# Loading one branch's output weights in 20 pieces instead of one in a two-branch attention decode kernel

## The chip, the cores and the metric

The kernel runs on one core of a Trainium2 chip. The core has five engines with their own instruction streams: TensorE (PE in the profile, its weight loads PEld), VectorE (DVE), ScalarE (ACT), GpSimd (POOL) and SyncE (SP), and sixteen DMA engines that move data between the chip's memory (HBM) and the core's buffer (SBUF, 128 partitions). SP computes nothing here; it only issues loads. The metric is the device time of one execution in microseconds, lower is better; several executions are timed and the median is given.

## The reference, cut to what matters

Two attention branches, A and B, each decode one token for a batch of two: 32 heads of width 128 over a cache of 4096 keys and values, then an output projection. A gate mixes the two results. Everything is in 32-bit floats. The two branches have separate caches and weights but share the input `A_x`.

```python
def branch(x, k_cache, v_cache, wq, wo):          # x [2, 1, 512]
    q = (x @ wq).reshape(2, 1, 32, 128).transpose(0, 2, 1, 3)
    scores = einsum("bhqd,bhkd->bhqk", q, k_cache) * 128 ** -0.5
    p = softmax(scores)
    o = einsum("bhqk,bhkd->bhqd", p, v_cache)     # caches [2, 32, 4096, 128]
    return o.transpose(0, 2, 1, 3).reshape(2, 1, 4096) @ wo    # wo [4096, 512]

g = sigmoid((x * gate_w).sum(-1, keepdims=True))
out = g * branch_A + (1 - g) * branch_B
```

The four caches are 134 MB each and the four weight matrices 8.4 MB each, so about 570 MB are read once.

## The kernel before

A unit is one group of four heads of one batch entry; a branch has 16 of them, and there are 32 in all. A unit's keys and its values are 8.4 MB each: 128 partitions, each with 128 tokens of 128 numbers, which lie one behind the other in HBM (64 KB for a partition). There are three such buffers: `kt[0]` and `kt[1]` take turns for the keys, `vt` holds the values. The query weights come before the first unit and the output weights after the last ones, through the same `kt` buffers.

For each unit VectorE multiplies the keys with the query in place and sums over the width (L391, L394), finds the maxima, ScalarE takes the exponentials (L365), and TensorE multiplies them with the values (L369). The loops of a branch run over pairs of units, one for each `kt` buffer. At the end of a branch the heads are gathered and scaled, and TensorE multiplies them with the output weights: branch A's in `project_out` (L489, products on L497) into the accumulator `most`, while the last unit of branch B is still under way; branch B's in `project_out` for the first 28 of 32 rows and in `project_last` (L508, products on L512) for the last four.

All large loads are issued by SP in an order that is written out (from L516): query weights A, keys 0, query weights B, keys 1, values 0, and then keys and values in turn. The last entries are keys 31, values 30, output weights A (`load_wo("A")`, L524), values 31, output weights B. `S.dma` (L97) issues one load and returns the semaphore count that says it has landed; each load adds 16 to the semaphore of its slot. Before a load SP waits until its buffer is free: for the output weights of A until VectorE is through with keys 30 (`k_free`), for values 31 until ScalarE reports that TensorE is through with values 30 (`v_free`), for the output weights of B until VectorE is through with keys 31. SP's instructions run strictly in order, so a load that is held up holds up those behind it.

The output weights are laid out as `(p r) e -> p r e`: partition p holds 32 rows (`OR`) of 512 numbers, 2 KB each, and these 32 rows lie one behind the other in HBM. `load_wo` (L243) loads branch A's in one piece, slot `f`, and branch B's in six pieces, slots `abchij`, with 16, 8, 4, 2, 1 and 1 rows of each partition. `parts` keeps the counts to wait for; `arrived` (L213) makes an engine wait for them. For branch A `project_out` waits once, for `parts["wo", "A"][0]`, ahead of its first product. The values of the last unit come in three pieces of 64, 48 and 16 tokens of each partition, and `last_products` (L381) waits for each in turn.

The end of the kernel: TensorE's products with branch B's output weights, a copy of the accumulator by ScalarE (L609), a product that folds it in (L612), copies out (L620, L621) and two small stores.

Of the kernel before, what the change touches and what calls it, by code (L numbers as in the profile page):

```python
# [12 lines left out]
P = 128  # L13
B = 2
# [14 lines left out]
OR = H * DH // P  # L29
DQ = DH // OR  # L30
EARLY = OR - 4
OS = 2
SCALE = DH ** -0.5

QUARTERS = [slice(j * PH, (j + 1) * PH) for j in range(G)]

# [9 lines left out]
class Streams:  # L46
# [32 lines left out]
    def put(self, e, make, reads=(), writes=(), gives=None):  # L79

        self.before(e, reads, writes)
        i = make(self.engines[e])
        if gives is not None:
            i.then_inc(gives, 1)
            return None
        self.ticks[e] += 1
        i.then_inc(self.sems[e], 1)
        point = self.sems[e], self.ticks[e]
        self.after(point, reads, writes)
        return point  # L90
# [51 lines left out]
def tile_gated_decode(ctx: ExitStack, tc: tile.TileContext, ins: dict, out: bass.AP):  # L142
# [12 lines left out]
    slot = small.tile([P, VC], F32, name="slot")  # L155
# [23 lines left out]
    with tc.tile_critical():  # L179
        S = Streams(nc, tc)  # L180
# [27 lines left out]
        parts = {}  # L208

        def load_parts(item, t, src, slots, *cuts):  # L210
            parts[item] = [S.dma("sp", t[:, i:j], src[:, i:j], slot=s) for s, i, j in zip(slots, cuts, cuts[1:])]
# [31 lines left out]
        def load_wo(n):  # L243
            i = place["wo", n]
            nc.sync.wait_ge(k_free[i], NU // 2)
            t = kt[i].rearrange("p r d -> p (r d)").rearrange("p (r e) -> p r e", e=D)
            for r in r_kt[i]:
                r.writers, r.readers = [], []
            load_parts(("wo", n), t, ins[n + "_wo"].rearrange("(p r) e -> p r e", p=P), *(
                ("f", 0, OR) if n == "A" else ("abchij", 0, OR // 2, 3 * OR // 4, EARLY, OR - 2, OR - 1, OR)))  # L250


        class Scratch:
# [8 lines left out]
        rows, ident, ones, xg, w, e = start(D), start(P), start(1), start(B * KC), start(P), start(1)  # L262
# [3 lines left out]
        def vput(e, make, reads=(), writes=(), **kw):  # L266
# [6 lines left out]
                                  slot="y"))  # L273
# [51 lines left out]
        def project(n):  # L325
# [20 lines left out]
            for i, t in enumerate(qa):  # L346
                half = slice(i * STRIPS * DH, (i + 1) * STRIPS * DH)
                mark(put("act", lambda x: x.activation(qrow[:, half], t.rearrange("p g d -> p (g d)"), AF.Copy, scale=SCALE),  # L348
                         [r_qa[i]], [r_qrow[i]]))
# [137 lines left out]
        wo = {}  # L487
# [33 lines left out]
        for u in range(2, NU):  # L521
            load_k(u)
            load_v(u - 1)
        load_wo("A")  # L524
        load_v(NU - 1)
        load_wo("B")

        spread_queries(0)
        for h in (0, 1):
            t = kt[0][:, h * NS // 2:(h + 1) * NS // 2]  # L530
            r = R()
# [84 lines left out]
        for i, e in enumerate(("dve", "act")):  # L616
            for j in range(STRIPS // OS):
                k = (i * STRIPS // OS + j) * QT
                src = acc[i][k:k + B, :D // STRIPS]
# [27 lines left out]
```

## Time and profile before

| what | value |
|---|---|
| median of 3 timed runs | 1324.44 us (1324.32 to 1324.47) |
| the profiled execution | 1324.58 us |
| its span (first to last instruction in the trace) | 1322.8 us |
| VectorE busy | 1166.3 us (88%) |
| TensorE busy | 343.3 us (26%) |
| ScalarE busy | 101.4 us (8%) |
| bytes read from HBM | 570.43 MB, 431 GB/s over the span |
| granted TensorE clock, mean | 0.627 |

The page of the profile lists the busy time of each engine, the span in 40 slices, the DMA queues, the chain of work that ended last and the costliest groups of instructions. Further views of the same trace give the busy time in chosen stretches, each engine's instructions in order of time, and who waited for whom. An engine's idle time costs nothing unless the chain that ends last passes through it. The DMA share of a stretch is the mean busy share of the sixteen DMA engines; in a very short stretch it can come out above 1.

### The profile page before, as it was taken

The page shows a single profiled execution, that of the slowest core. Times are in us where ns is not written, and L with a number is a line of the kernel's source. Part 1 is how long each engine was busy: PE and PEld are TensorE (multiplying, and loading weights), DVE is VectorE, ACT ScalarE, POOL GpSimd, SP SyncE. Part 2 cuts the span into 40 slices and gives each one's busy share as a digit, 9 for nine tenths or more (in the row PEclk, how much of TensorE's full clock was granted, in tenths as well). Part 3 has the DMA queues.
Part 4 walks back from the last instruction along what each step waited for, and adds up shares of the span by engine and source line. Part 5 has one row for each costly group of instructions (what it writes and reads, how often), then busy time and mean ns, then how long its engine had stood idle before and what let it go on. Part 6 is the DMA issues. An engine that isn't in the chain of part 4 may idle for free. (4 is left out here: it accounts for less than half of the span.)

```text
span 1322.8 us, 6257 instructions
## 1 busy us (share of the span) xinstructions
PE 343.3 (26%) x2406; PEld 100.7 (8%) x2406; DVE 1166.3 (88%) x321; ACT 101.4 (8%) x331; POOL 1.2 (0%) x8
## 2 busy tenths in 40 slices
PE   3202222202222221222224022222212222221256
PEld 0000000000000000000002000000000000000012
DVE  2399999999999999999999899999999999999960
ACT  0000000001010000101000010100001010000100
POOL 0000000000000000000000000000000000000000
PEclk9656666556666655666665566666566666656668
DMA  9999999999999999999999999999999999999998
GB/s 412 442 414 442 442 416 442 444 414 444 442 430 428 442 442 416 442 442 416 444 442 419 438 442 434 426 440 440 420 440 440 420 442 442 426 432 442 434 420 357
DMA packets 11109, 570.53 MB, mean 431 GB/s; under 512 B 1239, under 2 KB 1243, under 8 KB 1630
## 3 DMA queue, kind: packets, MB, share of 16 engines
q1 hardware_dynamic: 11092, 570.43, 99.6%
q8 instruction: 4, 0.07, 0.0%
q14 instruction: 3, 0.02, 0.0%
q10 hardware_dynamic: 10, 0.01, 0.0%
HBM read 570.43 MB, written 0.00 MB: 431 GB/s over the span
## 5 line engine op out<-in xcount | busy, mean ns | idle before, releaser
L391 DVE TENSOR_TENSOR kt<-kt,q 128x16384 f32<-128x16384 f32 x31 | 534.0, 17226 | 56.1 <-DVEq L95 56.0
L394 DVE TENSOR_REDUCE sc<-kt 128x128 f32<-128x16384 f32 x31 | 533.8, 17220 | 1.1
L369 PE MATMUL vp<-vt,pr 128*32 128x512 f32 x2048 | 291.8, 733 | 919.3 <-PEq L95 918.5
L369 PEld LDWEIGHTS vp<-vt,pr 128*32 128x32 f32 x2048 | 80.3, 132 | 1129.3 <-issue 1126.9
L365 ACT ACTIVATE pr<-sc,nm 32x128 f32<-32x128 f32 x128 | 50.9, 398 | 160.0 <-ACTq L95 118.2
L431 ACT ACTIVATE pr<-nil 128x512 f32<-128x512 f32 x31 | 19.3, 624 | 426.4 <-ACTq L95 426.4
L452 ACT ACTIVATE vs<-vp,slot 128x128 f32 (+1 forms) x16 | 5.9, 368 | 451.6 <-ACTq L95 451.6
L339 PE MATMUL qa<-kt,cols 128*2 128x512 f32 x128 | 18.7, 741 | 22.9 <-DMA kt<-in_B_wq_dram 15.7
L365 ACT ACTIVATION_READ_ACCUMULATOR pr<-sc,nm (+1 forms) x128 | 23.5, 184 | 0.0
L350 DVE STREAM_TRANSPOSE kt<-kt 128x1024 f32<-128x1024 f32 x1 | 1.2, 1246 | 23.5 <-ACT kt L348 23.5
L415 DVE SCALAR_TENSOR_TENSOR vs<-vp,slot,vs 128x128 f32 (+1 forms) x45 | 15.8, 351 | 6.3 <-DVEq L95 5.3
L534 DVE TENSOR_REDUCE sc<-kt 128x64 f32<-128x8192 f32 x2 | 17.4, 8686 | 0.1
L533 DVE TENSOR_TENSOR kt<-kt,q 128x8192 f32<-128x8192 f32 x2 | 17.4, 8686 | 0.0
L459 ACT ACTIVATE vp<-nil 128x512 f32<-128x512 f32 x15 | 9.0, 600 | 106.6 <-ACTq L95 106.6
L621 DVE COPY kt<-qa 2x128 f32<-2x128 f32 x2 | 0.6, 280 | 17.0 <-PE qa L512 17.0
L592 DVE TENSOR_REDUCE kt<-kt 128x32 f32<-128x128 f32 x1 | 0.4, 368 | 12.8 <-POOL kt L590 12.8
L497 PE MATMUL most<-kt,onA 128*2 128x512 f32 x64 | 8.6, 698 | 9.5 <-DMA kt<-in_A_wo_dram 9.5
L399 DVE TENSOR_REDUCE rm<-sc 128x1 f32<-128x128 f32 x31 | 8.7, 282 | 2.3
L405 DVE STREAM_TRANSPOSE q<-qsel 128x128 f32<-128x128 f32 x30 | 9.3, 311 | 1.3 <-DVE qsel L404 0.3
L602 DVE SCALAR_TENSOR_TENSOR vs<-vp,slot,vs 128x128 f32<-128x128 f32 x3 | 1.1, 352 | 10.6 <-DVEq L95 10.6
L350 DVE STREAM_TRANSPOSE vt<-vt 128x1024 f32<-128x1024 f32 x1 | 1.2, 1246 | 9.4 <-ACT vt L348 9.4
L497 PE MATMUL most<-kt,kt 128*2 128x512 f32 x56 | 8.6, 779 | 2.4 <-DMA kt<-in_B_wo_dram 2.4
(68 smaller groups left out, 72.9 us busy)
## 6 DMA issues: line engine op xcount, KB each, us to landing
kt<-in_A_wq_dram SPq DMA_DIRECT2D x2, 4096.0 KB, 16.6
kt<-in_A_k_cache_dram SPq DMA_DIRECT2D x2, 4096.0 KB, 29.0
vt<-in_B_v_cache_dram SPq DMA_DIRECT2D x1, 4096.0 KB, 18.3
kt<-in_B_wo_dram SPq DMA_DIRECT2D x1, 4096.0 KB, 33.1
vt<-in_B_v_cache_dram SPq DMA_DIRECT2D x1, 3072.0 KB, 25.2
kt<-in_B_wo_dram SPq DMA_DIRECT2D x1, 2048.0 KB, 37.5
vt<-in_B_v_cache_dram SPq DMA_DIRECT2D x1, 1024.0 KB, 27.2
kt<-in_B_wo_dram SPq DMA_DIRECT2D x1, 1024.0 KB, 39.5
```

The costliest lines, as they stand in the source:

```text
L339: put("pe", lambda x: x.matmul(t[h * QT:h * QT + B], cols[:, c], halves[:, c, i, h], start=c == 0, stop=c == KC - 1), [r_cols, *r_kt[i_k]] ...
L365: do(lambda x: x.activation(padded[h, :, b, j * VC:(j + 1) * VC], s[h].rearrange("p (c a) -> p c a", a=VC), AF.Exp, bias=m[h], accum_out=l ...
L369: return x.matmul(vp[c % STRIPS * QT:(c % STRIPS + 1) * QT], padded[:, c].rearrange("p b m -> p (b m)"), vt[:, c * VC:(c + 1) * VC].rearra ...
L391: at = D_.do(lambda x: x.tensor_tensor(kt[o], kt[o], q[:, None, :].to_broadcast([P, NS, DH]), op=ALU.mult), after)
L394: at = D_.do(lambda x: x.tensor_reduce(sc[o], kt[o], axis=AX.X, op=ALU.add), at)
L405: return D_.do(lambda x: x.transpose(q, qsel[:, 0].to_broadcast([P, DH // QT, QT])), at)
L415: at = D_.do(lambda x: x.scalar_tensor_tensor(vs[:, g], vp[:, a * DH:(a + 1) * DH], slot[:, a:a + 1], vs[:, g], op0=ALU.mult, op1=ALU.add) ...
L431: return A_.do(lambda x: x.activation(padded[:, :, b], nil[:, :, None].to_broadcast([P, NVC, G * VC]), AF.Copy))
L459: A_.do(lambda x: x.activation(vp, nil.to_broadcast([P, VC * DH]), AF.Copy))
L497: put("pe", lambda x: x.matmul(most[s * QT:s * QT + B], on[n][:, r], wo[n][:, r], start=n == "A" and r < STRIPS, stop=n == "B" and r >= EA ...
L533: put("dve", lambda x: x.tensor_tensor(t, t, q[:, None, :].to_broadcast([P, NS // 2, DH]), op=ALU.mult), [r_q], [r])
L534: put("dve", lambda x: x.tensor_reduce(sc[0][:, h * NS // 2:(h + 1) * NS // 2], t, axis=AX.X, op=ALU.add), [r], [R()])
```

## The change

Branch B's output weights load as before. Branch A's load in 20 pieces: first rows 0 to 24 of every partition in one load, then each of the rows 25 to 31 in two to four loads that take a run of partitions each. `SHARES` holds where a row is cut: row 25 at partition 120, row 26 at 104, row 27 at 126, row 28 at 110, row 29 at 100, row 30 at 112, 118, 123 and 127, row 31 at 117, 120 and 127. All 20 loads are issued by SP, one behind the other, at the place where the one load was, and all add to the semaphore of slot `f`; TensorE waits for the count of the last, which is that of all 20 together (320).

```diff
+SHARES = ((120,), (104,), (126,), (110,), (100,), (112, 118, 123, 127), (117, 120, 127))
...
             for r in r_kt[i]:
                 r.writers, r.readers = [], []
-            load_parts(("wo", n), t, ins[n + "_wo"].rearrange("(p r) e -> p r e", p=P), *(
-                ("f", 0, OR) if n == "A" else ("abchij", 0, OR // 2, 3 * OR // 4, EARLY, OR - 2, OR - 1, OR)))
+            src = ins[n + "_wo"].rearrange("(p r) e -> p r e", p=P)
+            if n == "B":
+                load_parts(("wo", n), t, src, "abchij", 0, OR // 2, 3 * OR // 4, EARLY, OR - 2, OR - 1, OR)
+                return
+            first = OR - len(SHARES)
+            pieces = [S.dma("sp", t[:, :first], src[:, :first], slot="f")]
+            for r, cuts in enumerate(SHARES, first):
+                for i, j in zip((0, *cuts), (*cuts, P)):
+                    pieces.append(S.dma("sp", t[i:j, r], src[i:j, r], slot="f"))
+            parts["wo", n] = pieces[-1:]
```

## The prediction

> **What bounds the kernel now.** I read the page's queue table first, then busy shares by stretch, then the chain of waits in order of time, then the last two microseconds of the transfers in short stretches.
>
> The queue table of the page (queue and kind: packets, MB, share of the sixteen DMA engines' span):
> ```profile
> span 1322.8 us, 6257 instructions
> ...
> q1 hardware_dynamic: 11092, 570.43, 99.6%
> ...
> q10 hardware_dynamic: 10, 0.01, 0.0%
> ```
> Queue q1, which SP fills, holds the engines for 99.6% of the span. VectorE, at 88%, is the only other busy engine. The busy times by stretch (after each engine's time come the clock, the DMA share and GB/s):
> ```profile
> 1.00:1316.00 1315.00, 340.00 (x2353) 99.63 (x2357) 1165.74 (x319) 100.21 (x328) 0.95 (x4) 0.62 1.00 433
> 1316.00:1317.00 1.00, 1.00 (x16) 0.28 (x12) 0.00 (x0) 0.00 (x0) 0.00 (x0) 1.00 1.02 399
> ```
> From 1 to 1316 us the sixteen engines never stand still (share 1.00). So the kernel is a single stream of 570 MB, and its end comes when the slowest of sixteen queues has handed over its last byte. Nothing that ends before that decides the time. The last bytes are branch B's output weights; the chain of waits, in order of time (start, us, what), shows them:
> ```profile
> 1276.21 33.05 DMA kt<-in_B_wo_dram
> 1309.27 0.04 issue
> 1309.31 8.70 PE most L497 x56
> 1318.01 0.02 issue
> 1318.03 0.61 ACT kt L609
> 1318.64 0.04 issue
> 1318.68 0.40 PE qa L612 x8
> 1319.09 0.56 PE qa L512 x16
> 1319.64 0.02 issue
> 1319.66 0.28 ACT kt L620
> ```
> TensorE starts on the first half of these weights when it lands (1309.3) and finishes at 1318.0; the last piece lands at about 1319.1, from these rows (an issue at 1278.6, 40.5 us to landing):
> ```profile
> L104 SPq DMA_DIRECT2D kt<-in_B_wo_dram x6: 328/429/2326, 1276.2 to 1278.6; - x6
> ...
> kt<-in_B_wo_dram SPq DMA_DIRECT2D x2, 256.0 KB, 40.5
> ```
> Both ends hang on the stream: if it comes 1 us later, both come 1 us later, and the 3.7 us from 1319.1 to the span's end follow unchanged. What matters to this change is how the sixteen engines finish. The DMA share by fifths of a microsecond:
> ```profile
> 1317.00:1317.20 0.20, 0.20 (x8) 0.00 (x0) 0.00 (x0) 0.00 (x0) 0.00 (x0) 1.00 0.90 348
> 1317.20:1317.40 0.20, 0.20 (x8) 0.00 (x0) 0.00 (x0) 0.00 (x0) 0.00 (x0) 1.00 0.54 205
> 1317.40:1317.60 0.20, 0.20 (x8) 0.00 (x0) 0.00 (x0) 0.00 (x0) 0.00 (x0) 1.00 0.45 174
> 1317.60:1317.80 0.20, 0.20 (x4) 0.00 (x0) 0.00 (x0) 0.00 (x0) 0.00 (x0) 1.00 0.27 102
> 1317.80:1318.00 0.20, 0.19 (x9) 0.11 (x8) 0.00 (x0) 0.00 (x0) 0.00 (x0) 1.00 0.30 113
> 1318.00:1318.20 0.20, 0.20 (x12) 0.20 (x8) 0.00 (x0) 0.17 (x1) 0.00 (x0) 1.00 0.24 92
> 1318.20:1318.40 0.20, 0.20 (x12) 0.01 (x2) 0.00 (x0) 0.20 (x1) 0.00 (x0) 1.00 0.29 113
> 1318.40:1318.60 0.20, 0.11 (x4) 0.00 (x0) 0.00 (x0) 0.20 (x1) 0.00 (x0) 1.00 0.09 31
> 1318.60:1318.80 0.20, 0.12 (x6) 0.11 (x9) 0.00 (x0) 0.03 (x1) 0.00 (x0) 1.00 0.06 20
> ```
> About half of the engines are done by 1317.3. From 1317.6 to 1318.4 the mean share is 0.275, so about four of sixteen still work; the last one stops near 1318.8. The shares add up to 3.14 × 0.2 = 0.63 us, so the mean engine ends at 1317.63. Dealing the remaining work perfectly evenly would bring the end from 1318.8 to 1317.63. **The most that any re-dealing can gain is 1.2 us.** The view does not tell which four engines are the late ones.
>
> **The change, part by part.** The same 8.4 MB load in the same place in the queue. One load of 128 partitions × 32 rows becomes one load of 25 rows per partition and 19 loads of 1 to 126 partitions × one 2 KB row. Bytes, buffers and order are as before, and all 20 loads raise one semaphore, which TensorE still awaits in full.
>
> *Issue on SP.* SP's own instructions (start, us, instruction, count):
> ```profile
> 1237.61 0.33 SPq L104 DMA_DIRECT2D kt<-in_A_wo_dram  x1
> 1271.57 1.28 SPq L104 DMA_DIRECT2D vt<-in_B_v_cache_dram  x3
> 1276.21 4.70 SPq L104 DMA_DIRECT2D kt<-in_B_wo_dram  x6
> ```
> At 0.43 us each (1.28/3, and the median 429 ns above), 20 issues take 8.6 us, 1237.6 to 1246.2. Queued behind them on SP are the three loads of branch B's last V tile, which wait for ScalarE until 1271.6 in any case. So the cost is nothing, hidden by 25 us of SP's waiting. If SP is held up past that, the V loads are late next; that is a rival below, because one issue in the rows above took 2326 ns.
>
> *Small rows.* A 2 KB share passes an engine in 16 × 2048 B / 433 GB/s = 75.7 ns in the long stretch, and in 16 × 2048 / 399 = 82.1 ns in the stretch from 1316 to 1317, which holds 4 KB and 2 KB rows with their semaphore writes. For an engine with 56 such rows (7 rows × 128 partitions / 16) that is 4.24 us before and 4.60 after: +0.36 us if the rows are still dealt evenly.
>
> *Who gets the rows.* Not shown for such loads. One bound is the even deal. The other: equal shares, which need a number of engines that divides the number of rows. The largest divisors up to 16 are 15 for 120, 13 for 104, 14 for 126, 11 for 110, 10 for 100, 16 for 112 and 13 for 117, and 8, 12, 2, 9, 14, 6, 5, 4, 1, 3, 7, 1 for the others. The nearest row speaks for it: q10, ScalarE's queue, has 10 packets for loads of 2, 1 and 2 rows, so five rows and five semaphore writes: each row had an engine to itself, and no engine without rows took part. I also take it that shares begin at the same engine each time; the other end, a start that moves round, comes out near the even deal. By this deal the engines get, first to last, 76, 74, 73, 72, 71, 70, 69, 68, 67, 65, 55, 45, 43, 26, 15 and 7 rows in place of 56. In time: the first 76 × 82.1 ns = 6.24 us, +2.0; the tenth 65 rows, +1.1; the eleventh +0.3; the twelfth −0.5; the last 0.57 us, −3.7.
>
> [...]
>
> *What that does to the end.* Behind this load come 16.8 MB of V and weights, 38.7 us at 433 GB/s, dealt evenly and queued well ahead: an engine that is d later after this load stays d later to the end, and nobody takes over its work. The new end is the largest of old end plus d. If one of the four late engines (ends 1318.4 to 1318.8) is among the first ten, whose mean is 70.5 rows or +1.55 us, the end is 1319.6 to 1320.8; I take 1318.65 + 1.55 = 1320.2, which is **1.4 us later**. If all four were among the last six, the first engine would still set 1317.3 + 2.0 = 1319.3 or more, 0.3 to 0.8 us later. The last engines' 3.7 us bring nothing: the mean engine ends as before.
>
> *TensorE.* Its wait for this load becomes 1.4 to 2 us longer:
> ```profile
> PE most L497 <- DMA kt<-in_A_wo_dram: 9.5, 1, 9.5
> ...
> PE most L497 <- DMA kt<-in_B_wo_dram: 2.4, 1, 2.4
> ```
> Behind it stand 8.6 us of products, the gathers and the last V products; the 2.4 us that TensorE later waits for branch B's weights cover it, and those weights are themselves late by as much. So nothing is added.
>
> *Sum.* Span 1322.8 + 1.4 = 1324.2. The profiled execution took 1324.58, 1.8 more than its span, and the median 1324.44 is 0.14 below that: 1324.2 + 1.8 − 0.1 = **1325.8 us**, 0.1% slower.
>
> **The rivals.**
>
> *SP is held up by full queues (slower).* The sixth load of branch B's weights took 2326 ns to issue, against 429. It was the tenth unfinished load (this one, three of V, six), and it came free at 1280.9 (1278.6 + 2.3), just after branch A's weights had landed (TensorE starts on them at 1280.2). If nine loads may be unfinished, SP issues seven pieces behind the two cache tiles in flight, two more as those land, and stands until the 25-row piece lands, at about 1280.2 − 4.2 = 1276.0. Eleven issues are then left, 4.7 us, and the first V load goes out at 1281.1. Meanwhile the last engines run dry. How long an empty engine takes to start, the first load shows (SP's row, then two stretches):
> ```profile
> 0.96 0.87 SPq L104 DMA_DIRECT2D kt<-in_A_wq_dram  x2
> ...
> 1.50:2.00 0.50, 0.00 (x0) 0.00 (x0) 0.00 (x0) 0.22 (x1) 0.18 (x1) 1.00 0.46 139
> 2.00:2.50 0.50, 0.00 (x0) 0.00 (x0) 0.00 (x0) 0.50 (x1) 0.00 (x0) 1.00 2.97 852
> ```
> Issued at 0.96, it moves bytes on most engines from 2.0 to 2.5: 1 to 1.5 us. So all engines restart at 1282.1 to 1282.6, and with 38.7 us the bytes end at 1320.8 to 1321.3, or 1321.6 with issues a little dearer: 2.0 to 2.8 us later than 1318.8, so 1326.4 to 1327.2. Against it: the limit may be one of entries per engine, with only 8 or 9 per large load; then SP is free again near 1278 and only the last engines, which have 3.7 us to spare, wait. The 2326 ns may also have another cause. This rival decides once SP issues the V loads after about 1280.
>
> [...]
>
> *Dealt evenly, or late engines all among the last.* +0.3 to +0.8 us by the two sums above: 1324.7 to 1325.2. For it: nothing shows where shares begin. Against it: four late engines placed by chance all fall among the last six in 15 of 1820 ways, so only a reason for their place would do it.
>
> *The deal hits the late engines (faster).* The gain ends at 1.2 us: 1323.3 to 1324.3. For it: a few engines are late by 1.0 to 1.2 us against the mean. Against it: that is 13 to 16 rows, where the deal takes up to 49 from one engine and gives 20 to another.
>
> *The change doesn't deal as said.* If loads whose rows do not divide by 16 went through one engine, that engine would get 791 rows, 65 us, and the time would be about 1385. The q10 row speaks against it.
>
> **How the numbers follow.** Forecast (0.9 to 2.0 us later) 0.50; SP held up 0.27; even deal or late engines last 0.13; faster deal 0.07; a coarser deal 0.03. What a measurement of this kernel can tell from no change is about 0.2%, 2.65 us, so up to 1327.09. No case but a mistake of mine gets below 1321.8: faster 0.03. Above 1327.09 lie somewhat less than half of the second case, the coarser deal, the forecast with issues dearer than 0.43 us each, and unforeseen losses: slower 0.30. Same 0.67. The range, 1324.2 to 1327.8, leaves out most of the gain and the coarse deal.
>
> **What would show it.** SP's rows: 20 issues for branch A's weights from 1237.6, done by 1246 (forecast) or still going after 1276 (first rival). The V loads at 1271.6, or after 1280. TensorE's wait for these weights 1.4 to 2 us longer than 9.5. The DMA share's tail: under the forecast a spread from below 1316 to about 1320.2, wider than now, because the last three engines end 2 to 3.7 us early; under the first rival a stretch of low share near 1277 to 1282 and a short, even tail. An end before 1318.5, or a tail as narrow as now, makes the deal, or its price, wrong.

## The result, and the profile after

The changed kernel takes 1330.16 us (median of 5 runs, 1329.70 to 1330.22) against 1324.47 before: 1.0042 times as long, interval 1.0027 to 1.0057, or 5.7 us more. The forecast was 1325.8 us with a range up to 1327.8, so the result lies outside it. The profiled execution has a span of 1328.4 us, 5.6 more than before.

The page's queue table of the changed kernel (packets, MB, share of sixteen engines):
```profile
span 1328.4 us, 6276 instructions
...
q1 hardware_dynamic: 12152, 570.43, 99.6%
```
The same bytes move, with the engines as busy as before, in 1060 packets more than the 11092 before. That number is telling: it is 896 rows of 2 KB (7 × 128) and 164 semaphore writes (packets under 512 B: 1403 against 1239). By the forecast's supposition, equal shares on the largest number of engines up to 16 that divides a load's rows, the 19 small loads use 15 + 8 + 13 + 12 + 14 + 2 + 11 + 9 + 10 + 14 + 16 + 6 + 5 + 4 + 1 + 13 + 3 + 7 + 1 = 164 engines, which with one semaphore write each is the measured number. With sixteen writes for every load it would have been 304. So the total is the one that the forecast supposed; it does not show the engines of a single load.

The chain of waits (start, us, what) has its old form, all of it moved:
```profile
1276.24 38.67 DMA kt<-in_B_wo_dram
...
1314.95 8.74 PE most L506 x56
...
1323.71 0.61 ACT kt L618
...
1324.36 0.40 PE qa L621 x8
1324.76 0.56 PE qa L521 x16
```
Branch B's weights were issued at the same time, 1276.2, and their first half landed 5.6 us later (1314.9 against 1309.3). The delay is there already when branch A's weights land. Waits of TensorE (total us, times, longest):
```profile
PE most L506 <- DMA kt<-in_A_wo_dram: 15.4, 1, 15.4
...
PE most L506 <- DMA kt<-in_B_wo_dram: 2.3, 1, 2.3
```
The first wait grew from 9.5 to 15.4 us, +5.9; the second hardly changed (2.4 before). So the whole loss has arisen by the time the changed load lands, and what follows only passes it on. Busy times by stretch, first one stretch of the kernel before, then the changed kernel (the last three numbers are clock, DMA share and GB/s):
```profile
1274.00:1285.00 11.00, 4.77 (x32) 0.93 (x36) 2.81 (x4) 1.96 (x8) 0.00 (x0) 0.57 0.90 388
```
```profile
1270.00:1274.00 4.00, 0.17 (x4) 0.00 (x0) 4.00 (x1) 0.63 (x1) 0.00 (x0) 1.00 0.97 410
1274.00:1285.00 11.00, 0.00 (x0) 0.00 (x0) 2.83 (x4) 1.96 (x8) 0.00 (x0) 0.57 1.06 265
1286.00:1316.00 30.00, 22.30 (x168) 8.81 (x164) 2.05 (x8) 0.96 (x3) 0.50 (x2) 0.84 0.99 427
```
From 1274 to 1285, while the small rows pass, the engines are fully busy (share 1.06) and move 265 GB/s; ahead of it and behind it they move 410 and 427. The view counts a packet, which is one transfer of one engine, whole in the stretch where it begins, so share and GB/s of a short stretch are read together: the kernel before has 388 GB/s at a share of 0.90, which is 431 at a share of 1, the changed kernel 265 at 1.06. This is the line to read: a share near 1 with little throughput. The engines did not run dry, and each transfer took longer. Eleven microseconds at 265 instead of 433 GB/s are worth 11 × (1 − 265/433) = 4.3 us.

SP's instructions (start, us, instruction, count):
```profile
1237.63 37.14 SPq L105 DMA_DIRECT2D kt<-in_A_wo_dram  x20
1274.81 1.30 SPq L105 DMA_DIRECT2D vt<-in_B_v_cache_dram  x3
1276.24 13.16 SPq L105 DMA_DIRECT2D kt<-in_B_wo_dram  x6
```
The 20 issues took 37.1 us instead of the 8.6 of the forecast, and the V loads went out 3.2 us late (1274.8 against 1271.6). The rival "SP is held up by full queues" had come true in its first step. Whether it cost the time was the first question for the experiments.

### The profile page after: what moved, and what is told of

Same layout as the page of the kernel before. It is cut to its first block, busy times and chain, and to the rows that moved or that the text cites. A ratio compares the mean times of both kernels' runs of the same rounds, so it can differ in the third digit from the quotient of the medians.

```text
span 1328.4 us, 6276 instructions
## 1 busy us (share of the span) xinstructions
PE 344.0 (26%) x2406; PEld 99.7 (8%) x2406; DVE 1166.3 (88%) x321; ACT 101.3 (8%) x331; POOL 1.2 (0%) x8
## 2 busy tenths in 40 slices
DMA packets 12169, 570.53 MB, mean 429 GB/s; under 512 B 1403, under 2 KB 1407, under 8 KB 2690
## 5 line engine op out<-in xcount | busy, mean ns | idle before, releaser
L506 PE MATMUL most<-kt,onA 128*2 128x512 f32 x64 | 8.8, 711 | 15.4 <-DMA kt<-in_A_wo_dram 15.4
```

The lines of the kernel that those rows point to most:

```text
L506: put("pe", lambda x: x.matmul(most[s * QT:s * QT + B], on[n][:, r], wo[n][:, r], start=n == "A" and r < STRIPS, stop=n == "B" and r >= EA ...
```

## The experiments

Four theories stood. **Shared groups** (the "port theory" of the expectations below)**:** engines that write to the same group of partitions at a time slow each other, which a load of all 128 partitions avoids and a load of fewer does not. The groups are the author's supposition: no run shows them, and which partitions would share one is open. **Rows:** 2 KB rows that lie 64 KB apart in HBM are slow to read. **Loads:** each further load costs its engines a fixed time. **Uneven deal:** only the number of rows for an engine counts, as in the forecast. The edits are to the changed kernel, or to the one before where that is said, and touch only the load of branch A's weights.

**Seven rows, each in one load of all 128 partitions.**
```diff
-SHARES = ((120,), (104,), (126,), (110,), (100,), (112, 118, 123, 127), (117, 120, 127))
+SHARES = ((),) * 7
```


> The last seven rows each as one load of all 128 partitions (8 loads in place of 20); same bytes, same 2 KB rows. Port theory (the sixteen engines are slow when a load of fewer partitions makes several of them write the same group of partitions): no slowdown, each 2 KB share about 82 ns instead of 76, so +0.4 us on before, about 1324.9. Row theory (2 KB rows that lie 64 KB apart in memory are slow to read): as slow as the changed kernel, about 1329 to 1330. Load theory (every extra load costs its engines a fixed time, 5.7 us over 19 extra loads): seven extra loads, +2.1, about 1326.6. Uneven-deal theory (only the unequal number of rows costs): the deal is even, about 1324.9.

Measured: 1324.88 us, 1.0002 times the kernel before (0.9993 to 1.0011). As shared groups and the uneven deal had it; the rows and loads theories asked for 2 us or more. Its stretches and SP's instructions:
```profile
1274.00:1285.00 11.00, 4.38 (x24) 0.84 (x28) 2.88 (x4) 1.96 (x8) 0.00 (x0) 0.50 1.05 434
...
1237.67 13.11 SPq L105 DMA_DIRECT2D kt<-in_A_wo_dram  x8
```
The same 896 rows of 2 KB pass at 434 GB/s. SP is held up here too, 13.1 us for eight issues, at no cost.

**Each row in two loads of 64 partitions.**
```diff
+SHARES = ((64,),) * 7
```


> Each of the seven rows in two loads, partitions 0 to 63 and 64 to 127 (15 loads); every engine gets four rows of each load, so the deal is even. Port theory: a load reaches half of the partition groups, so a 2 KB share takes up to twice 80 ns: 56 x 160 = 9.0 us instead of 4.2, up to +4.7, about 1327 to 1329.2. Row theory: as the run with 128 partitions a load. Load theory: 14 extra loads, +4.2, about 1328.7. Uneven-deal theory: about 1324.9.

Measured: 1328.40 us, 1.0030 (1.0018 to 1.0042), 3.9 us above the kernel before, inside the span that shared groups gave (up to +4.7), and near the +4.2 of the loads theory, which the run before had contradicted. The deal is even: 28 rows in the first half, 28 in the second, for every engine (the page counts 12212 packets, 1120 more than before, which is 896 rows and 14 × 16 semaphore writes). So the uneven deal is not needed for most of the loss. Nor is a late V load: SP issued the first at 1271.4, as before.
```profile
1274.00:1285.00 11.00, 0.62 (x4) 0.11 (x8) 3.12 (x4) 1.96 (x8) 0.00 (x0) 0.59 1.05 306
```

**The seven rows of a partition in one run of 14 KB, partitions 0 to 119 and 120 to 127 (3 loads).**
```diff
-            for r, cuts in enumerate(SHARES, first):
-                for i, j in zip((0, *cuts), (*cuts, P)):
-                    pieces.append(S.dma("sp", t[i:j, r], src[i:j, r], slot="f"))
+            for i, j in ((0, 120), (120, P)):
+                pieces.append(S.dma("sp", t[i:j, first:], src[i:j, first:], slot="f"))
```


> The last seven rows in two loads only, partitions 0 to 119 and 120 to 127, each partition's seven rows in one run of 14 KB (3 loads). Deal: fifteen engines get 8 runs, the first eight of them one more, the last none. [...] Row theory and load theory: no 2 KB rows and only two extra loads, so only the ninth run counts, +0.5, about 1325 to 1325.5. Uneven-deal theory: the same, about 1325.

Measured: 1331.29 us, 1.0051 (1.0035 to 1.0066), 6.75 us above the kernel before: slower than the changed kernel, with two extra loads in place of 19 and none of the 2 KB rows.
```profile
1274.00:1285.00 11.00, 0.00 (x0) 0.00 (x0) 2.71 (x4) 1.96 (x8) 0.00 (x0) 0.50 1.01 206
...
1237.51 1.17 SPq L105 DMA_DIRECT2D kt<-in_A_wo_dram  x3
1271.66 1.60 SPq L105 DMA_DIRECT2D vt<-in_B_v_cache_dram  x3
```
SP is not held up (three issues in 1.17 us, the V loads on time), and the rate is the lowest of these four runs. This excludes the loads theory and shows that the loss does not need SP's delay. The packet records of the trace, which hold every transfer's start, duration and size, show two things more. A run of 14 KB took 1057 ns on average, where an engine's even part of 433 GB/s makes it 530: twice as long, as if two engines at a time held each other up. And one engine got no such run from either load; it went on to the next V tile at 1274.2, and its first four packets there took 2.2 to 3.6 us each, where 1.2 is usual.

**The changed kernel's loads, reading rows that lie side by side in HBM.**
```diff
+            src = ins[n + "_wo"].rearrange("(r p) e -> p r e", p=P)
             for r, cuts in enumerate(SHARES, first):
```


> The 20 loads of the changed kernel, but the 19 small ones read rows that lie next to each other in memory, 2 KB apart instead of 64 KB (so seven eighths... of the products use the right weights only in the first 25 rows; the last seven rows hold other rows' weights). Port theory and load theory: as the changed kernel, about 1330.2. Row theory: fast again, the forecast's 1325.8 from the uneven deal alone.

Measured: 1329.88 us, 1.0040 (1.0025 to 1.0055), against 1330.16 for the changed kernel, and 264 GB/s against 265:
```profile
1274.00:1285.00 11.00, 0.00 (x0) 0.00 (x0) 2.87 (x4) 1.96 (x8) 0.00 (x0) 0.53 1.05 264
```
For these loads it makes no difference whether the rows lie 64 KB or 2 KB apart in HBM; the rows theory is out.

**Same number of loads, same bytes, other partitions.** The last four runs vary the partitions written to, and with them the rows read, as partition p's rows lie at p × 64 KB in HBM. From the kernel before, branch A's load is cut to 21 rows, and 11 loads of eight partitions follow, one row each:
```diff
+            first = OR - 11
+            parts["wo", n] = [S.dma("sp", t[:, :first], src[:, :first], slot="f")]
+            for r in range(first, OR):
+                parts["wo", n] = [S.dma("sp", t[0:85:12, r], src[0:85:12, r], slot="f")]
```
with `0:128:16` and `0:8` in the next two, and without the loop in the base.

> Only the first 21 of 32 rows of branch A's output weights are loaded, in one load (the products use whatever stands in the rest of the buffer). The base for the next three. 11 rows x 8 partitions x 75.7 ns = 6.7 us less for every engine: about 1317.9 on every theory, if the stream still bounds the end.

> As the base, with 11 small loads behind it: one 2 KB row each of the eight partitions 0, 12, 24, ..., 84 (the other 120 partitions' rows 21 to 31 are left out). Eight engines get 11 rows each. [...] Any theory that charges small loads or uneven deals as such: the same for this run and the next two.

> As before with partitions 0, 16, 32, ..., 112 in place of 0, 12, ..., 84: same number of loads, rows, bytes and engines. [...]

> [...] Port theory: a share takes 320 ns, 3.5 us, about 2.6 above the run with step 12. Other theories: equal to it.

| partitions of the 11 loads | median us (lowest to highest) | above the base |
|---|---|---|
| none (base) | 1319.08 (1318.47 to 1319.37) | |
| 0, 12, ..., 84 | 1319.80 (1319.46 to 1320.15) | 0.7 |
| 0, 16, ..., 112 | 1320.40 (1319.71 to 1320.93) | 1.3 |
| 0 to 7 | 1321.46 (1321.09 to 1321.87) | 2.4 |

The last is clear of the others; the middle two overlap in time. Steps 16 and 1 are 0.6 and 1.7 us above step 12, where every theory that charges small loads or uneven deals as such had the same time for all three. The expected 2.6 for step 1 came from a row of 320 ns on average, the author's estimate, which no run shows: it was 191. The base is 1.2 us above its expected 1317.9. Part of it is that the stream is no longer unbroken: by the packet records up to three engines stood without a transfer between 1271.6 and 1272.8, just after the V loads went out, and with steps 12 and 1 up to six did. How much of the 1.2 us this makes was not worked out. The throughput separates all of them. The stretch from 1271.5 to 1275, first the base, then step 12, step 16 and step 1:
```profile
1271.50:1275.00 3.50, 1.37 (x12) 0.36 (x16) 3.50 (x1) 0.00 (x0) 0.00 (x0) 0.87 1.11 437
```
```profile
1271.50:1275.00 3.50, 0.09 (x4) 0.09 (x8) 3.50 (x1) 0.00 (x0) 0.00 (x0) 0.61 1.02 363
```
```profile
1271.50:1275.00 3.50, 0.00 (x0) 0.00 (x0) 3.50 (x1) 0.00 (x0) 0.00 (x0) 1.00 1.04 263
```
```profile
1271.50:1275.00 3.50, 0.00 (x0) 0.00 (x0) 3.50 (x1) 0.00 (x0) 0.00 (x0) 0.65 0.98 173
```
The shares are all near 1 or above, at 437, 363, 263 and 173 GB/s. With each packet spread over its time in place of counted where it begins, the rates are 374, 329, 271 and 173: the order stays. The packet records give the price of one 2 KB row directly:
```
2 KB rows of branch A's weights, ns      count  mean  least  most
128 partitions a load                      896    84     84    84
64 partitions a load                       896   125     84   253
changed kernel                             896   138     84   352
changed kernel, rows side by side in HBM   896   138     84   320
8 partitions, step 12                       88    85     84   131
8 partitions, step 16                       88   124     84   207
8 partitions, step 1                        88   191     84   345
```
A row takes 84 ns in loads of all 128 partitions, and 85 on average at step 12. At step 16 the longest takes 207, at step 1 345. With steps 16 and 1, 40 and 33 of the 88 rows still took 84: presumably the engines reach these loads at different times and do not always meet, which would also be why the row of step 1 came out below 320 on average. In the changed kernel only 79 of 896 rows took 84.

One rival is not fully excluded: these runs also read from other places in HBM. The slowest, step 1, reads rows 64 KB apart, as the run with 128 partitions a load does at 84 ns, so there the distance is not the cause. For step 16, whose rows lie 1 MB apart, no run separates the two.

## Why the prediction was wrong, point by point

**The bound was right.** The stream alone sets the end: TensorE's second wait stayed at 2.3 us (2.4 before), and the delay at the first landing appears at the end. The even deal in 128-partition loads gave +0.3, where the forecast's 2 KB price for such loads gives +0.36; a difference so small is not clear of zero. No run tested the ceiling of 1.2 us.

**The deal fits.** The 1060 extra packets fit the supposed engines of the 19 loads in total, and the run with 14 KB runs has 151 more packets than the kernel before (11243 against 11092), its 128 runs and 15 + 8 semaphore writes. Which engine got how many rows, from 76 down to 7 in the forecast, no run shows. That the shares begin at the same engine each time fits as well: in the run with 14 KB runs the engine that the first load left out got nothing from the second either. Whether the late engines are among those that come first was not tested.

**The step that failed is "small rows".** A 2 KB share was put at 82.1 ns for every load, taken from the last pieces of branch B's weights. Those pieces have 128 partitions each, and the runs show that the price does not hold for every load: 84 ns there and 85 on average at step 12, but 125 in loads of 64 partitions and 138 in the changed kernel. With 138, the 76 rows supposed for the first engine take 10.5 us in place of 4.24, +6.2 us; TensorE's wait grew by 5.9 and the median by 5.7. So the term was too small by a price that came out two thirds higher. That the sum with 138 comes so near the measured loss is partly luck: it takes the loss for the first engine's alone, and the next paragraph shows that most of it fell on all. The forecast's bounds, 75.7 and 82.1 ns, came from two stretches filled by loads of 128 partitions; neither said anything of a load that leaves partitions out.

**"The mean engine ends as before" fell with it.** In the forecast an engine that gets fewer rows simply ends earlier; the last one, with 49 rows less, was put at −3.7 us. The changed kernel's tail by microseconds:
```profile
1319.00:1320.00 1.00, 1.00 (x12) 0.20 (x8) 0.00 (x0) 0.00 (x0) 0.00 (x0) 0.57 0.93 369
1320.00:1321.00 1.00, 1.00 (x16) 0.23 (x12) 0.00 (x0) 0.00 (x0) 0.00 (x0) 1.00 0.89 365
1321.00:1322.00 1.00, 1.00 (x12) 0.19 (x8) 0.00 (x0) 0.00 (x0) 0.00 (x0) 1.00 0.66 264
1322.00:1323.00 1.00, 1.00 (x16) 0.20 (x8) 0.00 (x0) 0.00 (x0) 0.00 (x0) 1.00 0.54 211
1323.00:1324.00 1.00, 1.00 (x24) 0.32 (x16) 0.00 (x0) 0.29 (x1) 0.00 (x0) 1.00 0.28 109
1324.00:1325.00 1.00, 0.70 (x28) 0.49 (x24) 0.00 (x0) 0.31 (x1) 0.00 (x0) 1.00 0.03 10
```
Nothing ends below 1316, as the forecast's last engines should have: the share from 1316 to 1319 stays between 0.95 and 1.01. The shares add up to 3.33 us, so the mean engine ends at 1322.3, against 1317.63 before: 4.7 us later for the same work. The last end is some 5.6 us later. So about 4.7 us of the loss fall on the mean engine, and about 1 us is the wider spread. The packet records account for the 4.7: the 896 rows at 138 in place of 75.7 ns make 3.5 us for each of sixteen engines, and the 128 packets of 32 KB that begin the next V tile, 1376 ns on average and up to 2978 where it was 1215 before, make 1.3. The second part is how engines with few rows lost time as well; that others held them up at the partitions they wrote to fits this and is an inference.

**SP held up: it happened and was not the cause.** The rival set its point of decision at V loads issued after 1280; they went out at 1274.8. The 13.1 us of issuing without loss and the 1.17 us with the largest loss show both halves. In the changed kernel SP's 3.2 us of delay left one engine without a transfer, for about a microsecond at most: the packet records have at times fifteen packets in progress between 1275.0 and 1276.0, never fewer, and sixteen or more from there to 1290.

**Partitions, not the number of loads.** Seven pairs of 64 partitions cost 3.9 us, and two further loads of 14 KB runs 6.75. The runs speak for the partitions that a load writes to as the reason, not for the number of loads.

**TensorE's cover and the copies at the end** came as forecast: nothing was added behind the stream.

## What to carry to other kernels

Price a transfer from rows of the same shape: the number of partitions, and which ones, belong to the shape as much as the bytes do (a 2 KB row took 84 ns in loads of all 128 partitions and 191 on average in loads of partitions 0 to 7). In a kernel bound by its loads, a DMA share near 1 is no proof of full rate (here 1.06 at 265 GB/s); read GB/s beside it, in the stretch that changed. Balancing sixteen engines by loads of fewer partitions cost here several times what perfect balance could have brought, 1.2 us.

## What the runs showed of the hardware

- The rate of a load depended on the partitions that it wrote to. With eight partitions to each small load and the same bytes, the core moved 363, 263 or 173 GB/s at steps of 12, 16 and 1 between partitions, and 14 KB runs on partitions 0 to 119 and 120 to 127 brought the whole core to 206 GB/s, where seven loads of all 128 partitions passed at 434. That engines slow each other at shared groups of partitions fits these figures and is an inference; for step 16 the distance of the rows in HBM, 1 MB, was not separated from it.
- SP can be held up in issuing. Eight loads of 128 partitions took 13.1 us, the 20 of the change 37.1, with about two 8.4 MB loads queued ahead, and in the kernel before the last of branch B's six took 2326 ns. A limit on unfinished loads alone does not fit: one issue of the change began at 1241.7 and ended at 1249.9 us, and no load landed between 1241.5 and 1260.9. What the limit is stays open.
